# Linear attention and a gated feed-forward layer on one core: the first 900 steps in a new order, and a last store on another queue

## The chip, the cores and the metric

The kernel runs on one core of one Trainium2 chip. The metric is the device time of one execution, in microseconds (us); the profile is of one execution of its own. In the profile PE is TensorE's matrix unit (PEld its weight loads), DVE is VectorE, ACT is ScalarE, POOL is GpSimd and SP is SyncE, which here only issues transfers.

## The reference

Eight heads of linear attention make x, and x goes through a gated feed-forward layer. Cut to what is computed:

```python
# q, k, v: (8 batches, 8 heads, 576 rows, 64)
q_s = softmax(q, over the 64)            # exp(q - max) / (sum + 1e-9)
k_s = softmax(k, over the 576 rows)
kv  = einsum('bhsd,bhse->bhde', k_s, v)
x   = einsum('bhsd,bhde->bhse', q_s, kv) # to (4608 tokens, 512)
xn  = x / sqrt(mean(x * x) + 1e-6) * rms_g
g   = xn @ w_gate                        # (512, 1536)
out = (g * sigmoid(g) * (xn @ w_val)) @ w_out
```

## The kernel before

The 4,608 tokens are nine blocks of 512. The first three (j = 0, 1, 2) go through the layer one after the other, the last six in pairs, by Strassen's products. All products are in float32r: an operand is split into a high and a low part, and three products are added. One program on one core does all of it, and its whole order is written out by hand: `ORDER` is a string of 3,337 steps such as `k_tr.0.2` or `q_sub0.0.3:P`, each a small function with its indices; a letter behind the colon sets the engine (S, A, D, P for SyncE, ScalarE, VectorE, GpSimd). Each engine works through its own instructions in that order, and semaphores hold it where an operand is not ready. Transfers are issued by SP in the same order, a few by ScalarE.

The steps that matter here, with their lines:

- `constants` (435) fills the identity and `mean_w` on GpSimd; `warm` (473) issues TensorE products of `mean_w` that nothing reads. I call them idle products.
- k's softmax needs the maximum over rows. `k_load` (494) loads a pair of heads (b, g); `k_max0` (544, batch 0) or `k_max` (541) take maxima on VectorE; `k_tr` (550, line 554 or 557) turns them on TensorE; `k_top` (560) reduces them on VectorE; `k_rows` (564) turns the result back over all rows; `k_sub` (573) and `k_exp` (577) follow, `k_mm` (588 or 594) multiplies by v with a column of ones, and `k_eps` (612), `k_rec`, `kv_norm0` or `kv_hi` (620) and `kv_lo` divide by the sum. `v_load` (525, 529, 530) loads v, and `kv_zero` (610), `kv_zero0` (606) and `v_ones` (534, 536, 537) fill tiles on GpSimd.
- q's softmax in blocks 0 and 1: `q_load0` (678), `q_max0` (684), `q_sub0` (688), `q_exp` (751), `q_sum0` (693), `q_eps0` (423 or 421), `q_rec0` (700), `q_mul0` (704), `q_t0` (711, four turnings on TensorE), `q_c0`, `q_x0` (724). In block 2 the steps are `q_max` (730), `q_half` (735), `q_max2` (743), `q_sub` (747), `q_sum` (761), `q_half2`, `q_sum2`.
- `n_y0`, `n_y1` (873 to 875, nine small VectorE operations, 128x16 each) and `n_rows` (879) make 1/rms of a block.
- The layer: `load_w` (450), then `conv_mul`, `conv_low`, `conv_shift`, `conv_add` turn weights from float64 words to float32; `w_hi`, `w_lo` (922), `o_hi`, `o_lo` (930) split them; `f1.s.a` (1005) is 12 products into one of two `ps_gv` buffers for chunk s = 12 j + i, with a = 0 for the gate and 1 for the value; `g_mul` (1010) and `h_mul` (1017) read them on VectorE and so free them, `silu` (1014) stands between; `f2` (1042) multiplies by `w_out` into the four `ps_o` banks. `w_keep`, `o_keep`, `s_keep` (990) and `store` (1049) issue transfers out.
- The end: `e_add`, `e_tr`, `e_copy` (409) and `e_put` (1443) bring the last four quarter tiles, 128 KB each, to the output.

The tiles of k have two buffers (`kt`), so a `k_load` waits until the `k_mm` two loads before it has read its tile:

```python
kt = ap.tile([KP, 2, CH, D], F32, name="kt")   # bufs=2
```

Of the kernel before, what the change touches and what calls it, by code (L numbers as in the profile page):

```python
# [27 lines left out]
v_load.0.2 q_eps0.0.1:A q_sub0.0.0:P q_exp.0.0 conv_mul.1.1 q_max0.0.3 k_rows.0.1 k_sub.0.1 q_sum0.0.0 k_exp.0.1
q_exp.0.2 q_eps0.0.0:D k_mm.0.0 k_eps.0.0:D conv_shift.1.1 warm.2.23 q_rec0.0.1 q_mul0.0.1:P conv_low.0.1.1 k_load.1.0
load_w.0.2 warm.2.11 q_rec0.0.0 k_sub.0.3 k_exp.0.3 k_rec.0.0 warm.2.12 q_sum0.0.2 q_eps0.0.2:A k_rows.0.2 k_sub.0.2  # L30
q_load0.1.0 v_ones.0.3 k_mm.0.1 k_eps.0.1:A conv_mul.0.1 warm.2.21 q_sub0.0.3:D load_w.2.1 k_rec.0.1 warm.2.22
q_rec0.0.2 q_exp.0.3 load_w.1.0 warm.2.5 k_mm.0.3 q_mul0.0.0:P q_t0.0.0 conv_mul.0.0 q_load0.1.1 load_w.3.0 load_w.2.0
q_mul0.0.2:P kv_norm0.0.0:D k_exp.0.2 k_eps.0.3:A q_t0.0.1 conv_low.0.0.1 kv_norm0.0.1:D conv_shift.0.1 conv_add.0.1.1
conv_shift.0.0 load_w.4.1 load_w.1.2 q_c0.0.0:A kv_zero0.1 q_sum0.0.3 q_eps0.0.3:D warm.2.13 q_rec0.0.3 q_c0.0.1:A
q_load0.1.2 k_mm.0.2 k_eps.0.2:A conv_mul.0.2 q_x0.0.0 k_max.1.0 conv_add.0.0.1 k_rec.0.3 kv_norm0.0.3:D warm.2.24
load_w.4.0 w_hi.0.0.2:A x_sq.0.0 k_tr.1.0 q_mul0.0.3:D q_t0.0.3 load_w.3.2 q_c0.0.3:A q_x0.0.1 k_rec.0.2 q_max0.1.0
kv_norm0.0.2:D conv_low.0.2.1 conv_shift.0.2 q_t0.0.2 x_hi.0.0:A q_x0.0.3 k_top.1.0 k_rows.1.0 w_lo.0.0:P x_hi.0.1:D
x_lo.0.1 q_c0.0.2:A q_sub0.1.0:P q_exp.1.0 warm.2.25 x_sq.0.3 k_sub.1.0 x_lo.0.0 conv_add.0.2.1 q_max0.1.1 x_sq.0.1
q_x0.0.2 x_sq.0.2 kv_zero.5 q_sum0.1.0 conv_mul.1.0 conv_shift.1.0 w_lo.0.1:P x_hi.0.2:A x_lo.0.2 q_sub0.1.1:P
x_hi.0.3:A n_sum0.0 q_eps0.1.0:A x_lo.0.3 n_sum0.1 kv_zero.1 n_sum0.2 n_sum0.3 warm.2.9 f1.0.0.0.0 f1.0.0.0.1  # L40
v_load.1.0 conv_low.1.0.2 q_rec0.1.0 conv_add.1.0.2 kv_zero.7 f1.0.0.0.2 f1.0.0.0.3 f1.0.0.1.0 k_exp.1.0 q_mul0.1.0:P
conv_mul.2.0 f1.0.1.0.0 f1.0.0.1.1 f1.0.1.0.1 o_hi.0:A conv_low.2.0.2 load_w.3.1 f1.0.0.1.2 o_lo.0:P k_load.1.1
f1.0.1.0.2 w_hi.1.0.2:A w_lo.1.0:P n_t.0 n_y0.0 f1.0.0.1.3 f1.0.0.2.0 f1.0.1.0.3 conv_low.1.2.1 conv_shift.2.0
f1.0.0.2.1 f1.0.0.2.2 f1.0.1.1.0 f1.0.0.2.3 conv_mul.2.1 n_y1.0 n_rows.0 g_mul.0 conv_shift.2.1 f1.0.1.1.1 f1.0.1.1.2
f1.0.1.1.3 conv_mul.1.2 load_w.2.2 conv_shift.1.2 conv_add.1.2.1 f1.0.1.2.0 f1.0.1.2.1 f1.0.1.2.2 k_load.1.2
w_lo.1.1:D kv_zero.0 f1.1.0 q_exp.1.1 conv_mul.4.0 q_sum0.1.1 conv_mul.4.1 conv_shift.4.1 g_mul.1 f1.0.1.2.3 silu.0
k_mm.1.0 conv_shift.4.0 q_eps0.1.1:A k_eps.1.0:D o_hi.1:A conv_mul.3.0 conv_add.2.0.2 load_w.6.0 h_mul.0 q_rec0.1.1
f1.1.1 h_hi.0:A q_t0.1.0 w_hi.2.0.2:A h_lo.0:P load_w.6.1 f2.0 load_w.5.1 k_rec.1.0 kv_norm0.1.0:D conv_mul.3.1 silu.1
q_mul0.1.1:P load_w.4.2 q_c0.1.0:A conv_shift.3.0 conv_low.3.0.2 w_lo.2.1:D q_max0.1.2 conv_shift.3.1 w_lo.2.0:D
f1.2.0 q_load.2.0 conv_mul.2.2 conv_low.4.0.2 conv_add.3.0.2 kv_zero.3 q_sub0.1.2:D exp_table o_lo.1:P conv_mul.6.0  # L50
w_hi.3.0.2:A h_mul.1 w_lo.3.0:P h_hi.1:A h_lo.1:P conv_add.4.0.2 q_exp.1.2 load_w.5.0 conv_shift.2.2 kv_hi.1.0:D
k_max.1.1 w_lo.3.1:P g_mul.2 q_x0.1.0 x_hi.1.0:D q_sum0.1.2 silu.2 x_lo.1.0 q_eps0.1.2:D conv_low.2.2.1 conv_shift.6.0
conv_mul.6.1 conv_shift.6.1 conv_mul.3.2 q_load0.1.3 x_sq.1.0 f1.2.1 h_mul.2 conv_low.4.2.1 conv_mul.5.1
conv_add.2.2.1 conv_shift.3.2 load_w.7.1 f2.1 conv_shift.5.1 q_rec0.1.2 f1.3.1 load_w.7.0 conv_low.3.2.1
conv_add.3.2.1 q_max.2.0 v_load.1.1 conv_mul.4.2 conv_shift.4.2 kv_zero.6 o_hi.2:A o_lo.2:D q_half.2.0 q_mul0.1.2:P
f1.3.0 load_w.5.2 q_max0.1.3 load_w.8.1 h_hi.2:A h_lo.2:D conv_mul.5.0 k_tr.1.1 conv_shift.5.0 g_mul.3 k_top.1.1
w_hi.4.0.2:A w_lo.4.0:D w_lo.4.1:D conv_low.6.0.2 conv_mul.7.0 q_max2.2.0 conv_shift.7.0 conv_low.5.0.2 o_hi.3:A
# [1429 lines left out]
```

## Time and profile before

| | us |
|---|---|
| median of 3 runs (932.59 to 933.10) | 932.92 |
| the profiled execution itself | 932.95 |
| its span, first to last instruction | 930.7 |
| TensorE busy (99% of the span) | 920.5 |
| VectorE busy (78%) | 727.0 |
| GpSimd busy (56%) | 522.4 |
| ScalarE busy (50%) | 461.4 |

2.25 us of the profiled execution lie outside the span. In the profile's 40 slices of 23.3 us TensorE shows 8 in the first and the last and 9 (90% or more) in all the others, and the granted clock is 9 throughout; the chain of work that ended last is TensorE for 95% and VectorE for 3%. A share over the whole says little here: what idle time TensorE has stands in a few places, and the rows of the section below are taken from them.

### The profile page before, as it was taken

Reading aid. Unit: us, or ns where it says so; the run is one execution under the profiler, and the core shown is the slowest. Engines: PE = TensorE matmul, PEld = TensorE weight load, DVE = VectorE, ACT = ScalarE, POOL = GpSimd, SP = SyncE. Lnnn points to the kernel's source line nnn. Section 1 sums busy time; section 2 is a strip of 40 time slices with the busy share of each in tenths; the row PEclk is TensorE's granted clock in tenths of the full one; section 3 lists DMA queues with packets and bytes.
Section 4 is the critical chain, followed back from the end, with each engine's and each line's share of the span. In section 5 each row is a group of like instructions: output and inputs, shape, how many; then the busy total and the mean of one; then the engine's idle time right before and its main releaser. Section 6 shows DMA issues by size and latency. Waiting matters only on the chain.

```text
span 930.7 us, 14213 instructions
## 1 busy us (share of the span) xinstructions
PE 920.5 (99%) x4621; PEld 748.1 (80%) x4621; DVE 727.0 (78%) x1520; ACT 461.4 (50%) x741; POOL 522.4 (56%) x539
## 2 busy tenths in 40 slices
...
GB/s 266 281 268 195 161 90 252 316 275 323 244 221 188 257 246 244 253 255 210 246 211 204 240 274 277 280 304 284 202 184 182 210 195 285 267 185 181 69 158 91
DMA packets 216569, 211.06 MB, mean 227 GB/s; under 512 B 138416, under 2 KB 177840, under 8 KB 211888
## 3 DMA queue, kind: packets, MB, share of 16 engines
...
q14 instruction: 36, 0.29, 0.1%
...
## 4 chain that ended last, share of the span: by engine, by line
PE 95%; DVE 3%; DMA 1%; issue 0%; ACT 0%; POOL 0%; DVEq 0%; ACTq 0%; POOLq 0%
PE ps_gv L1005 20%; PE ps_gv L1154 18%; PE ps_o L1154 12%; PE ps_o L1042 10%; PE ps_a L1154 7%; PE ps_o L1363 6%; PE ps_o L1247 4%; PE ps_a L1363 4%; PE ps_gv L1363 3%; PE ps_a L594 2%; PE ps_a L802 2%; PE ps_a L1247 2%; PE ps_gv L1247 2%; PE ps_o L802 1%; PE ps_gv L476 1%; DMA wd<-w 1%
## 5 line engine op out<-in xcount | busy, mean ns | idle before, releaser
L1005 PE MATMUL ps_gv<-xh,w 128*128 128x512 f32 x576 | 190.6, 397 | 1.3 <-DVE gs L1017 1.3
L1154 PE MATMUL ps_gv<-x,ring 128*128 128x512 f32 x576 | 143.0, 392 | 0.0
L1005 PEld LDWEIGHTS ps_gv<-xh,w 128*128 128x128 f32 x576 | 108.2, 188 | 26.0 <-DVE gs L1017 1.4
L1154 PEld LDWEIGHTS ps_gv<-x,ring 128*128 128x128 f32 x576 | 107.0, 188 | 23.0
L1005 PE MATMUL ps_gv<-xl,w 128*128 128x512 f32 x288 | 112.3, 391 | 0.0
L1175 DVE TENSOR_TENSOR tmp<-tmp,ps_gv 128x512 f32<-128x512 f32 x84 | 57.3, 684 | 49.6 <-PE ps_gv L1154 48.1
L1154 PE MATMUL ps_o<-x,ring 128*128 128x512 f32 x360 | 85.1, 389 | 0.0
L1127 POOL DMA_DIRECT2D ring<-wd x54 | 31.0, 575 | 91.3 <-PE ps_o L1154 34.1
L1154 PEld LDWEIGHTS ps_o<-x,ring 128*128 128x128 f32 x360 | 67.6, 188 | 14.2
L1042 PE MATMUL ps_o<-o,hh 128*128 128x512 f32 x288 | 73.1, 396 | 0.0
L1005 PEld LDWEIGHTS ps_gv<-xl,w 128*128 128x128 f32 x288 | 54.2, 188 | 10.6 <-issue 0.4
L1042 PEld LDWEIGHTS ps_o<-o,hh 128*128 128x128 f32 x288 | 53.0, 188 | 11.3 <-issue 0.4
L1175 DVE TENSOR_TENSOR tmp<-tmp,ps_o 128x512 f32<-128x512 f32 x42 | 28.7, 685 | 29.1 <-PE ps_o L1154 26.0
L409 ACT CAST hh<-gs 128x512 fp32r<-128x512 f32 x48 | 29.6, 616 | 31.7 <-DVE gs L1017 17.4
L1127 POOL DMA_DIRECT2D w<-wd x18 | 10.1, 559 | 58.2 <-PE ps_a L1154 37.9
L922 POOL TENSOR_TENSOR w<-w,w 128x512 fp32r<-128x512 f32 x29 | 39.3, 1363 | 5.1 <-ACT w L409 5.0
L1042 PE MATMUL ps_o<-o,hl 128*128 128x512 f32 x144 | 38.7, 391 | 0.0
L1154 PE MATMUL ps_a<-x,w 128*128 128x512 f32 x144 | 36.9, 392 | 0.0
L541 DVE TENSOR_REDUCE cm<-kt 128x128 f32<-128x640 f32 x28 | 36.7, 1310 | 0.1
L1154 PE MATMUL ps_a<-x,ring 128*128 128x512 f32 x144 | 36.7, 390 | 0.0
L1026 POOL TENSOR_TENSOR hl<-gs,hh 128x512 fp32r<-128x512 f32 x21 | 28.2, 1343 | 14.9 <-ACT hh L409 9.0
L1154 PE MATMUL ps_gv<-x,w 128*128 128x512 f32 x144 | 35.1, 391 | 0.0
...
## 6 DMA issues: line engine op xcount, KB each, us to landing
...
```

The lines of the kernel that those rows point to most:

```text
L409: (e.copy if e is nc.scalar else e.tensor_copy)(dst, src)
L541: nc.vector.tensor_reduce(out=cm, in_=kt_[b, g].rearrange("p h j d -> p h d j"), axis=AX.X, op=ALU.max)
L802: nc.tensor.matmul(px[:, c0:c1], lhsT=wt, rhs=mv[:, c0:c1], start=(i == 0), stop=(i == 2))
L922: on(nc.gpsimd).tensor_tensor(out=w[:, :, 1], in0=halves(CHUNK[s], a, 1)[:, 0], in1=w[:, :, 0].bitcast(F32), op=ALU.subtract)
L1005: nc.tensor.matmul(pd[s], lhsT=w[:, a, c // 2, m, c % 2 * P:c % 2 * P + P], rhs=X[j, c][x], start=(n == 1), stop=(n == 3 * NKT))
L1026: on(nc.gpsimd).tensor_tensor(out=hl, in0=g_[s], in1=h_[s][0].bitcast(F32), op=ALU.subtract)
L1042: nc.tensor.matmul(po[t], lhsT=a[:, t * P:(t + 1) * P], rhs=w, start=(i == 0 and n == 0), stop=(i == NF - 1 and n == len(terms) - 1))
L1127: nc.gpsimd.dma_start(t, src.rearrange("p a b f -> p (a b f)"))
L1154: nc.tensor.matmul(abc[p, i, m, b], lhsT=src[:, h, c * P:(c + 1) * P], rhs=operand(o, c, x), start=first and n == 0, stop=n == 5, skip_gro ...
L1175: nc.vector.tensor_tensor(out=dst, in0=ux[u + (src,)], in1=abc[u + (b,)], op=ALU.add)
L1247: nc.tensor.matmul(pa[p, t, k], lhsT=a[:, k * P:(k + 1) * P], rhs=w, start=(c == 0 and n == 0), stop=(c == NF - 1 and n == 2))
L1363: nc.tensor.matmul(qacc[p, b, x], lhsT=ws[l][x], rhs=h[m], start=first and i == 0 and n == 0, stop=i == NH - 1 and n == 2, skip_group_chec ...
```

## The change

`ORDER` is rewritten up to about step 900 of 3,337 (f1.18.0, near 200 us), and one step at the very end gets another engine. No step is added or left out, and the functions are the same; the string is one line longer, so every line number of the functions is higher by one. Of the table the diff shows the first lines and the last:

```diff
 ORDER = """
-kv_zero.4 k_load.0.0 v_ones.0.0 kv_zero0.0 g_load constants warm.2.2 warm.2.4 warm.2.7 warm.2.6 v_ones.1.1 k_max0.0.0
-warm.2.3 k_load.0.2 k_tr.0.0 k_top.0.0 k_max0.0.2 k_load.0.1 warm.2.8 k_max0.0.1 k_tr.0.2 warm.2.0 k_load.0.3
+q_load0.0.1 constants warm.2.2 warm.2.4 warm.2.6 k_load.0.0 k_load.0.2 warm.2.21 k_max0.0.0 warm.2.0 v_ones.0.0
+warm.2.3 k_max0.0.2 k_tr.0.2 k_top.0.2 k_tr.0.0 k_top.0.0 kv_zero.4 k_load.0.3 warm.2.7 g_load k_load.0.1 k_max0.0.3
...
-e_tr.0.0 e_tr.0.1 e_copy.0.0:A e_add.1.0 e_copy.0.1:A e_tr.1.0 e_put.0.0:S e_add.1.1 e_tr.1.1 e_put.0.1:S e_copy.1.0:D
+e_tr.0.0 e_tr.0.1 e_copy.0.0:A e_add.1.0 e_copy.0.1:A e_tr.1.0 e_put.0.0:S e_add.1.1 e_tr.1.1 e_put.0.1:A e_copy.1.0:D
 e_copy.1.1:A e_put.1.0:S e_put.1.1:S
```

These steps stand on another engine than before: q_sub0.0.3 and q_sub0.1.2 on GpSimd in place of VectorE; q_eps0.0.0, q_eps0.1.2, k_eps.1.1, k_eps.1.2, h_hi.7, h_hi.9 and x_hi.1.3 on ScalarE in place of VectorE; q_eps0.0.1, k_eps.0.1, q_eps0.1.1, h_hi.11, q_hi.2.0, kv_hi.2.0 and kv_hi.2.2 on VectorE in place of ScalarE; h_lo.10 on VectorE in place of GpSimd; e_put.0.1 on ScalarE's queue in place of SP's.

**TensorE, from its first instruction to the first product with v.** L476 are the idle products, L554 a k_tr (three turnings), L567 a k_rows, L588 a k_mm; `w_92` holds k's maxima. Before:

```order
L476 MATMUL ps_gv<-mean_w 128x512 x10
L554 MATMUL ps_o<-ident,w_92 128x96 x3
L476 MATMUL ps_gv<-mean_w 128x512 x2
L554 MATMUL ps_o<-ident,w_92 128x96 x3
L476 MATMUL ps_gv<-mean_w 128x512 x4
L567 MATMUL ps_o<-ident,kx 96x128
L554 MATMUL ps_o<-ident,w_92 128x96 x3
L476 MATMUL ps_gv<-mean_w 128x512 x2
L554 MATMUL ps_o<-ident,w_92 128x96 x3
L476 MATMUL ps_gv<-mean_w 128x512 x11
L567 MATMUL ps_o<-ident,kx 96x128 x2
L588 MATMUL ps_o<-w_93,w_94 64x128 x12
```

And with the change:

```order
L477 MATMUL ps_gv<-mean_w 128x512 x12
L555 MATMUL ps_o<-ident,w_92 128x96 x6
L477 MATMUL ps_gv<-mean_w 128x512 x4
L568 MATMUL ps_o<-ident,kx 96x128
L477 MATMUL ps_gv<-mean_w 128x512 x2
L555 MATMUL ps_o<-ident,w_92 128x96 x3
L477 MATMUL ps_gv<-mean_w 128x512 x13
L555 MATMUL ps_o<-ident,w_92 128x96 x3
L477 MATMUL ps_gv<-mean_w 128x512 x4
L568 MATMUL ps_o<-ident,kx 96x128
L477 MATMUL ps_gv<-mean_w 128x512 x2
L589 MATMUL ps_o<-w_93,w_94 64x128 x12
```

Twelve idle products stand ahead of the first turning in place of ten, two k_tr follow each other, and the last k_tr and the k_rows behind it have moved behind more of the idle products.

**VectorE, from block 1's 1/rms to k's second subtraction of batch 2.** L573 is a k_sub (`kt_1276` is head pair 2.0, `kt_1558` is 2.1), L873 to L875 are one of n_y1's three rounds (the other two are left out), L743 is q_max2.2.2, L879 n_rows.1, L562 k_top.2.1, L1010 g_mul.12. Before:

```order
L867 TENSOR_SCALAR y_1741<-ps_a_1680 128x16
L573 TENSOR_TENSOR kt_1276<-kt_1276,ps_a_1686 128x640
L873 SCALAR_TENSOR_TENSOR ps_a_1680<-y_1741,ps_a_1680 128x16
L874 TENSOR_TENSOR ps_a_1680<-ps_a_1680,y_1741 128x16
L875 SCALAR_TENSOR_TENSOR y_1741<-ps_a_1680,y_1741 128x16
L743 TENSOR_REDUCE sw_1774<-st_1571 128x16
L879 STREAM_TRANSPOSE r_1776<-y_1741 128x512
L562 TENSOR_REDUCE kx_1782<-ps_a_1769 128x1
L1010 TENSOR_TENSOR gs_1784<-ps_gv_1688,r_1776 128x512
L573 TENSOR_TENSOR kt_1558<-kt_1558,ps_a_1769 128x640
```

And with the change (`kt_1272` is 2.0, `kt_1595` is 2.1):

```order
L868 TENSOR_SCALAR y_1738<-ps_a_1674 128x16
L874 SCALAR_TENSOR_TENSOR ps_a_1674<-y_1738,ps_a_1674 128x16
L875 TENSOR_TENSOR ps_a_1674<-ps_a_1674,y_1738 128x16
L876 SCALAR_TENSOR_TENSOR y_1738<-ps_a_1674,y_1738 128x16
L574 TENSOR_TENSOR kt_1272<-kt_1272,ps_a_1683 128x640
L880 STREAM_TRANSPOSE r_1775<-y_1738 128x512
L1011 TENSOR_TENSOR gs_1777<-ps_gv_1690,r_1775 128x512
L762 TENSOR_REDUCE sum_1_1780<-qt_1306 128x16
L563 TENSOR_REDUCE kx_1785<-ps_a_1783 128x1
L574 TENSOR_TENSOR kt_1595<-kt_1595,ps_a_1783 128x640
```

n_y1 has moved ahead of k_sub.2.0, g_mul.12 ahead of k_top.2.1, and q_sum.2.1 has come in between.

**SP's queue, at the loads of k and v for batch 2.** L501 and L503 are a k_load (`kt_1825` is 2.2, `kt_1908` is 2.3), L529 and L530 a v_load, L990 a store of parts, L948 a w_keep, L952 an o_keep, L1049 a store of the output. Before:

```order
L501 DMA kt_1825<-in_k_dram 128x2x256
L503 DMA kt_1825<-in_k_dram 128x2x64
L990 DMA wd1_105<-parts_1723 128x2x512
L529 DMA vt_1845<-in_v_dram 128x4x64 x2
L530 DMA vt_1845<-in_v_dram 64x2x64
L1049 DMA out_0_dram<-ot_1860 128x512
L501 DMA kt_1908<-in_k_dram 128x2x256
L503 DMA kt_1908<-in_k_dram 128x2x64
```

And with the change (`kt_1827` is 2.2, `kt_1831` is 2.3):

```order
L502 DMA kt_1827<-in_k_dram 128x2x256
L504 DMA kt_1827<-in_k_dram 128x2x64
L949 DMA wd5_109<-w_1600 128x2x1024
L502 DMA kt_1831<-in_k_dram 128x2x256
L504 DMA kt_1831<-in_k_dram 128x2x64
L991 DMA wd1_105<-parts_1725 128x2x512
L1050 DMA out_0_dram<-ot_1868 128x512
L1050 DMA out_0_dram<-ot_1875 128x512
L953 DMA od11_121<-o_1679 128x1024
L530 DMA vt_1835<-in_v_dram 128x4x64 x2
L531 DMA vt_1835<-in_v_dram 64x2x64
```

k_load.2.3 now stands ahead of v_load.2.2, and so do two stores of the output and an o_keep.

## Rows read from the trace of the kernel before

**Rows 1.** Stretch, length; busy us of PE, PEld, DVE, ACT, POOL; clock, DMA, GB/s.
```profile
10.00:20.00 10.00, 10.00 (x84) 7.74 (x84) 9.69 (x20) 6.33 (x12) 5.88 (x8) 1.00 1.10 292
20.00:30.00 10.00, 8.83 (x77) 5.99 (x77) 9.55 (x24) 7.99 (x16) 7.54 (x7) 1.00 1.07 316
...
36.00:140.00 104.00, 104.00 (x530) 83.62 (x529) 90.37 (x176) 81.50 (x121) 86.06 (x74) 1.00 0.62 184
140.00:160.00 20.00, 17.96 (x113) 14.19 (x112) 16.97 (x47) 14.24 (x22) 13.26 (x17) 1.00 0.71 251
```

**Rows 2.** Timeline of POOL's first us: start, us, what, [idle before, releaser].
```profile
0.73 0.34 POOL L610 MEMSET kv<- 128x128 f32 x2 [0.29 <-POOLq L1472]
...
1.56 0.20 POOL masks.py:197 MEMSET ident<- 128x128 f32 x1
```

**Rows 3.** Timeline of PE: the first idle products.
```profile
2.33 4.64 PE L476 MATMUL ps_gv<-mean_w 128*128 128x512 f32 x10 [2.33 <-POOL vt L536]
```

**Rows 4.** Timeline of DVE, 3 to 27 us: k's maxima, q_sub0.0.3, a kv_norm0, q_mul0.0.3.
```profile
3.85 0.55 DVE L547 TENSOR_TENSOR w<-w 96x384 f32<-96x384 f32 x1 [3.85 <-DMA w<-in_k_dram]
7.49 0.46 DVE L562 TENSOR_REDUCE kx<-ps_o 128x1 f32<-128x288 f32 x1 [3.08 <-PE ps_o L554]
...
19.45 0.86 DVE L688 TENSOR_TENSOR r<-r,st 128x512 f32<-128x512 f32 x1
...
25.73 0.58 DVE L416 TENSOR_SCALAR ot<-ps_o,rs 64x64 f32<-64x64 f32 x2
26.32 0.69 DVE L704 TENSOR_TENSOR xl<-r,sm 128x512 f32<-128x512 f32 x1
```

**Rows 5.** Timeline of SP's issues: six of q's loads.
```profile
3.21 2.83 SPq L678 DMA_DIRECT2D qt<-in_q_dram  x6
```

**Rows 6.** Timeline of PE: q_t0.0.3, and the first real products.
```profile
27.16 0.63 PE L711 MATMUL ps_o<-ident,xl 128*128 128x128 f32 x4 [1.17 <-DVE rs L618]
...
35.56 1.07 PE L1005 MATMUL ps_gv<-xh,w 128*128 128x512 f32 x4
```

**Rows 7.** Timeline of PE, 150 to 158 us: k_tr.2.1, k_rows.2.1, k_mm.2.1, f1.13.1.
```profile
150.59 0.27 PE L557 MATMUL ps_a<-ident,cm 128*128 128x128 f32 x1
151.60 0.32 PE L567 MATMUL ps_a<-ident,kx 128*128 128x128 f32 x1 [0.74 <-DVE kx L562]
...
155.54 0.80 PE L594 MATMUL ps_a<-vt,kt 128*64 128x65 f32 x20
157.63 0.50 PE L1005 MATMUL ps_gv<-xh,w 128*128 128x512 f32 x1 [1.29 <-DVE gs L1017]
```

**Rows 8.** Timeline of DVE, 144 to 156; last, L922's min/median/max in ns, 36 to 160.
```profile
144.55 0.66 DVE L761 TENSOR_REDUCE sum<-qt 128x16 f32<-128x512 f32 x1
...
148.01 0.82 DVE L573 TENSOR_TENSOR kt<-kt,ps_a 128x640 f32<-128x640 f32 x1 [2.28 <-PE ps_a L567]
148.75 0.17 DVE L873 SCALAR_TENSOR_TENSOR ps_a<-y,ps_a 128x16 f32<-128x16 f32 x1
...
150.66 0.71 DVE L879 STREAM_TRANSPOSE r<-y 128x512 f32<-128x512 f32 x1
...
154.38 1.76 DVE L922 TENSOR_TENSOR w<-w,w 128x512 fp32r<-128x512 f32 x1
...
L922 DVE TENSOR_TENSOR w<-w,w x13: 677/693/1756, 41.7 to 154.4; 128x512 fp32r<-128x512 f32 x13
```

**Rows 9.** v_load.2.2's first issues, landing of v's six (156 to 170), k_mm.2.2.
```profile
156.77 1.97 SPq L529 DMA_DIRECT2D vt<-in_v_dram  x2
...
DMA to landing us min/median/max: 4.0/5.6/6.2
...
169.88 0.80 PE L594 MATMUL ps_a<-vt,kt 128*64 128x65 f32 x20
```

**Rows 10.** The last four issues on SP; ScalarE's own issues before, ns.
```profile
926.34 1.99 SPq L1443 DMA_DIRECT2D out_dram<-res  x4
...
L1409 ACTq DMA_DIRECT2D out_dram<-res x8: 322/430/672, 914.3 to 921.6; - x8
```

More of the change, by code (lines that the diff above doesn't have):

```diff
@@ L28 @@
[L28 to L57, printed above, removed]
@@ L83 @@
-silu.11 v_ones.2.0 v_load.2.0 q_load.2.3 o_hi.11:D n_sum.1 h_mul.11 o_lo.11:D kv_lo.1.2:P k_tr.2.0 f1.12.0 q_hi.2.0:A
-q_sub.2.1:P w_keep.12:S r_keep.5 kv_lo.1.3:P q_exp.2.1 f1.12.1 r_keep.2 s_add.1.1:D r_keep.0 n_t.1 s_add.1.2:P
-h_hi.11:A k_top.2.0 s_hi.1.1:A q_sum.2.1 h_lo.11:P k_rows.2.0 s_hi.1.2:A n_y0.1 f2.11 k_sub.2.0 n_y1.1 k_exp.2.0
-o_keep.12:S k_tr.2.1 store.0.0:A q_max2.2.2 n_rows.1 q_sub.2.2:P store.0.2:A k_top.2.1 g_mul.12 k_rows.2.1 s_lo.1.1:P
-k_mm.2.0 q_exp.2.2 k_sub.2.1 w_keep.13:S w_hi.14.0.2:A r_keep.1 f1.13.0 k_eps.2.0 q_half2.2.1 s_add.1.4:P k_load.2.2
```

184 lines of the change are left out of this document (110 added, 74 removed).

## The prediction, before the change was run

> **What bounds the kernel now.** I read the time by stretch first, then the early stretch engine by engine, then the one late stretch in which TensorE is idle, and last the end. By stretch [rows 1], TensorE is not idle at all from 10 to 20 us, for 1.17 between 20 and 30, not at all from 36 to 140 (104.00 of 104.00), and for 2.04 between 140 and 160. The reader should see that what the change reorders ends near 200 us, that TensorE's work is the same in both kernels, and that the time can therefore only move by TensorE's idle time in three places: before its first product (2.33 [rows 3]), before q's last turnings of the first block, and in 140 to 160. The granted clock is 1.00 in all these stretches; still the first ten products take 4.64 us [rows 3].
>
> At the start TensorE waits until 2.33 for POOL, which fills `kv`, a stripe of ones and `ot` (from 0.73) before it starts on the identity at 1.56 [rows 2, 3]. VectorE then sits idle for 3.08 us until k's first maxima are turned at 7.49 [rows 4]: its first maximum was done at 4.40, but the turning stood behind the ten idle products. From there to 27 us VectorE is the bound: 9.69 and 9.55 of 10 us busy [rows 1]. The 1.17 us that TensorE waits until 27.16 end with VectorE's chain, in which q_mul0.0.3 (26.32) is the last large piece [rows 4, 6]. From 27.16 to the first real product at 35.56 [rows 6] TensorE is almost without idle time, so that start moves with 27.16.
>
> **The change, part by part.** It leaves every step in, puts about the first 900 of 3,337 in a new order, and gives 18 another engine, one of them a store.
>
> *Start, POOL and TensorE.* The constants now come first on POOL: 1.56 less 0.73, 0.83 us earlier [rows 2], so the first idle product starts at about 1.50 in place of 2.33. But twelve idle products now stand ahead of the first turning, not ten: at 0.46 us each (4.64 by ten [rows 3]) that gives back 0.93, so TensorE comes to it at 7.0, as before. And two of q's loads are now issued ahead of k's on SP: at 0.47 each (2.83 for six [rows 5]) they put k's first landing from 3.85 to 4.8 or later [rows 4], and the first turning now needs the second k load, which lands after that. Gain here: nothing. VectorE does two k maxima ahead of its first reduction, not one, and is ahead by that one, 0.55 [rows 4]. I let it be lost again: thirteen idle products now stand ahead of k_tr.0.1, where two did since the turning before, and VectorE's k_eps.0.0 now waits for k_mm.0.0, which comes behind another six.
>
> *Start, VectorE.* Up to q_mul0.0.3 VectorE loses q_sub0.0.3 (0.86 [rows 4], to POOL) and gains k_eps.0.1 (some 0.15, as small as its other steps on one column); q_eps0.0.0 and q_eps0.0.1 swap engines and cancel. That is 0.71 us less in a chain that is full, so q_mul0.0.3 ends 0.7 earlier and TensorE's wait of 1.17 shrinks to about 0.5. POOL takes the subtraction where it is idle; its cover is gone if q_mul0's steps on POOL come later by it, at most the 0.86 itself. Bounds of the whole start: 0 if the idle products eat it, 2.0 (0.83 + 1.17) if TensorE's earlier start and the whole wait come through. I take **0.6**, near VectorE's 0.71, since its chain is what ends last there.
>
> *36 to 140.* No idle time before; the moved steps (q_sub0.1.2 to POOL, h_hi.7 and h_hi.9 to ScalarE, eps steps) cost nothing as long as TensorE's operands stay ahead of it. Where one doesn't, the price is a wait like those in the late stretch, 0.7 to 1.3 [rows 7]. I count 0 and let the range hold one half of such a wait.
>
> *140 to 160.* Before, VectorE stands idle for 2.28 us until k_rows.2.0 lets k_sub.2.0 run at 148.01, and only then does n_y1's nine small operations and one more (148.75 to 150.66); k_top.2.1 and g_mul.12 stand behind them [rows 8]. TensorE waits 0.74 for k_top.2.1, and 1.29 for h_mul.12, until 157.63 [rows 7]. Now the ten run inside the idle 2.28. k_top.2.1 can run as soon as k_tr.2.1 has (150.59 + 0.27), so the 0.74 falls to about 0.3. But f1.13.1 waits for h_mul.12, and from 148.01 to its release is 9.62 us: less 1.91 for the ten, plus q_sum.2.1 (0.66), plus kv_hi.2.0 as a pair on VectorE (0.58, as the pair in [rows 4]), plus q_max2.2.3 (some 0.17), plus about 0.6 of idle time for the trip k_tr, k_top, k_rows that was covered: 9.7. So h_mul.12 gains nothing by count, and the second wait grows by what the first loses. The other bound is w_lo.14.1: it took 1.76 where this operation's median on VectorE is 0.69 [rows 8]; if it runs undisturbed, h_mul.12 comes 1.07 earlier. I take **0.35**, nearer to the count.
>
> The row shows one subtraction of VectorE stretched by 1.07 us. The Trainium skill, SBUF — State Buffer, section "Who interferes with whom", says that a VectorE instruction with two SBUF inputs and a POOL instruction that reads SBUF take turns at a shared port. By that rule the stretch stays as long as POOL adds or subtracts at that time, which the new order still has it do, and this stage's gain would be 0.
>
> *The end.* e_put.0.1 goes to ScalarE's queue. The four last stores take 1.99 us of issuing on SP [rows 10]; with three there the last could be issued up to 0.5 earlier, but ScalarE must issue its store first (0.32 to 0.67 for its other stores [rows 10]) and only then makes the copy that the last store needs. I take **0.1**, bounds -0.2 and 0.5. The Trainium skill, DMA: Bandwidth & Descriptors, section "Issuing engines are not separate DMA queues", says that such a move saves issuing time only, as the transfers share the same engines; by that the end of the transfers would stay where the bytes put it, and the gain would be near 0.
>
> **Sum.** 0.6 + 0.35 + 0.1 = 1.05 us off the profiled execution's own 932.95, which lies 0.03 above the median of the three runs: **931.9 us**, 0.11% less. A measurement of this kernel tells about 0.2% from no change, 1.87 us: below 931.05 is faster, above 934.8 slower.
>
> **The rivals.**
>
> *Faster: TensorE alone is the bound of the start.* It starts 0.83 earlier and the whole wait of 1.17 goes, less some 0.5 for k's later landing: 1.5. w_lo.14.1 runs undisturbed: 1.0 in the late stretch. With the end 2.65: 930.3. For it: the idle products may hide waits that no row shows; against it: VectorE's 9.7 of 10 us.
>
> *No gain: it does not do what it says.* The order shows twelve idle products ahead of the first turning, and sixteen ahead of k_rows.0.0, as many as before; k lands later. Then 27.16 stays, the late stretch gives 0.1 and the end 0.1: 932.7.
>
> *Slower: SP's queue stands behind k_load.2.3.* It now comes ahead of a store of parts, two stores of the output, o_keep.13 and v_load.2.2, and its buffer is free only when k_mm.2.1 is done (155.54 + 0.80 [rows 7]). Before, v_load.2.2 was issued from 156.77 [rows 9]. The queue would go on at 156.4 with two k issues, the parts and three stores; at 0.5 to 1.0 an issue (0.99 for v's first two [rows 9]) v's three issues lie between 159.4 and 165.4, and the last lands 4.0 to 6.2 later [rows 9]: 163.4 to 171.6. k_mm.2.2 needs it at 169.88 [rows 9], 1 us sooner if the gains above come. It decides once v lands after that; at 171.6 TensorE stands 2.7 us, and if none of the gains come the time is 935.6, with them 934.6. I price it at 935.0. For it: issues are slow there; against it: the middle of the bounds, 167.5, is still in time.
>
> **How the numbers follow.** Forecast 0.48 (its own spread 931.0 to 932.8); faster rival 0.25; no gain 0.17; slower rival 0.10. Faster by over 0.2%: the faster rival and a little of the forecast's lower end, 0.27; slower: most of the slower rival, 0.09; same 0.64. The range leaves out the slower rival and the part of the faster one that lies below its price: 930.1 to 933.3.
>
> **What would show it.** Right: a first product near 1.5; a wait before q_t0.0.3 of about 0.5 and the first real product near 35.0; no idle time from there to 140; in the late stretch a wait of 0.3 before k_rows.2.1 and of 1.3 or more before f1.13.1. Wrong: a first real product before 34.3, or still at 35.5; a wait of TensorE in 36 to 140; a wait of k_mm.2.2 with v's load as its releaser; a w_lo.14.1 of 0.7.

## The result, and the profile after

The changed kernel takes **938.67 us** (median of six runs, 938.18 to 942.10) beside 933.01 for the kernel before in the same runs: a ratio of 1.0063, interval 1.0046 to 1.0080, so slower by 0.6%. The forecast was 931.9 in a range of 930.1 to 933.3. The profiled execution took 938.85 with a span of 936.7, so 6.0 us more span than before. In the later runs the executions of one kernel scatter by up to some 12 us on one chip, so below each ratio comes with its interval, and what an edit does is read from where TensorE's products start in the traces.

The page of the changed kernel, its busy times:

```profile
PE 923.0 (99%) x4621; PEld 748.3 (80%) x4621; DVE 732.6 (78%) x1521; ACT 460.8 (49%) x739; POOL 520.6 (56%) x540
```

The two later stretches of [rows 1], one more behind them, and three short ones (length; busy us of PE, PEld, DVE, ACT, POOL; granted clock, DMA, GB/s):

```profile
36.00:140.00 104.00, 102.92 (x518) 81.15 (x518) 91.77 (x171) 82.82 (x124) 81.21 (x68) 1.00 0.64 190
140.00:160.00 20.00, 18.54 (x116) 14.64 (x114) 17.11 (x39) 10.93 (x15) 15.47 (x22) 1.00 0.57 187
160.00:180.00 20.00, 17.80 (x92) 14.66 (x93) 17.34 (x47) 13.20 (x21) 11.51 (x11) 0.91 0.89 291
...
158.70:162.10 3.40, 0.23 (x8) 0.09 (x4) 3.26 (x8) 0.15 (x1) 2.90 (x4) 1.00 1.05 390
162.10:165.80 3.70, 3.60 (x9) 2.88 (x10) 3.53 (x15) 2.37 (x5) 1.54 (x3) 0.54 0.88 313
165.80:170.00 4.20, 4.20 (x20) 3.48 (x19) 2.75 (x5) 3.95 (x6) 3.46 (x3) 1.00 0.75 210
```

36 to 140 now holds 1.08 us in which TensorE is idle, where it held none. And there is something new: a stretch in which TensorE's clock is granted at about half, 0.54 from 162.1 to 165.8, right behind 3.3 us in which it did nothing.

Timeline of PE (start us, us, what, [idle before, releaser]); the lines that answer to [rows 3, 6, 7] and the two in between where it now waits:

```profile
1.50 4.74 PE L477 MATMUL ps_gv<-mean_w 128*128 128x512 f32 x12 [1.50 <-POOL mean_w L438]
7.20 0.71 PE L555 MATMUL ps_o<-ident,w 96*128 96x96 f32 x6 [0.95 <-DVE w L548]
...
27.41 0.63 PE L712 MATMUL ps_o<-ident,xl 128*128 128x128 f32 x4 [1.16 <-DVE xl L705]
...
69.22 0.32 PE L568 MATMUL ps_a<-ident,kx 128*128 128x128 f32 x1 [0.19 <-DVE kx L563]
...
115.32 1.19 PE L1043 MATMUL ps_o<-o,hl 128*128 128x512 f32 x4 [0.50 <-DVE hl L1027]
...
154.19 0.32 PE L568 MATMUL ps_a<-ident,kx 128*128 128x128 f32 x1 [0.39 <-DVE kx L563]
...
162.19 0.79 PE L1006 MATMUL ps_gv<-xh,w 128*128 128x512 f32 x1 [3.27 <-DVE gs L1018]
162.78 0.63 PE L1006 MATMUL ps_gv<-xl,w 128*128 128x512 f32 x1
163.21 0.63 PE L1006 MATMUL ps_gv<-xh,w 128*128 128x512 f32 x1
```

The last two lines start 0.43 apart. The same products before start 0.23 apart:

```profile
157.97 0.39 PE L1005 MATMUL ps_gv<-xl,w 128*128 128x512 f32 x1
158.20 0.40 PE L1005 MATMUL ps_gv<-xh,w 128*128 128x512 f32 x1
```

DVE and POOL in the trace of the changed kernel:

```profile
5.33 0.55 DVE L548 TENSOR_TENSOR w<-w 96x384 f32<-96x384 f32 x1 [5.33 <-DMA w<-in_k_dram]
6.59 0.55 DVE L548 TENSOR_TENSOR w<-w 96x384 f32<-96x384 f32 x1 [0.71 <-DMA w<-in_k_dram]
...
26.57 0.69 DVE L705 TENSOR_TENSOR xl<-r,sm 128x512 f32<-128x512 f32 x1
...
109.75 2.91 DVE L923 TENSOR_TENSOR w<-w,w 128x512 fp32r<-128x512 f32 x1 [1.19 <-ACT w L410]
...
114.58 0.68 DVE L1027 TENSOR_TENSOR hl<-gs,hh 128x512 fp32r<-128x512 f32 x1
...
157.76 2.72 DVE L923 TENSOR_TENSOR w<-w,w 128x512 fp32r<-128x512 f32 x1
160.51 0.69 DVE L736 TENSOR_REDUCE st<-st 32x16 f32<-32x16 f32 x4
161.23 0.19 DVE L744 TENSOR_REDUCE sw<-st 128x16 f32<-128x32 f32 x1
161.45 0.69 DVE L1018 TENSOR_TENSOR gs<-ps_gv,gs 128x512 f32<-128x512 f32 x1
```

```profile
109.57 1.29 POOL L931 TENSOR_TENSOR o<-w,o 128x512 fp32r<-128x512 f32 x1
110.82 1.29 POOL L923 TENSOR_TENSOR w<-w,w 128x512 fp32r<-128x512 f32 x1
...
157.43 2.50 POOL L979 TENSOR_TENSOR sums<-w 128x512 f32<-128x512 f32 x2
...
159.94 1.66 POOL L979 TENSOR_TENSOR sums<-w 128x512 f32<-128x512 f32 x1
```

w_lo.14.1 (157.76) takes 2.72 where it took 1.76 in [rows 8], and ends at 160.48, 0.55 behind the second of two POOL additions in a row (157.43 + 2.50 = 159.93). h_mul.12 (161.45) stands behind it, and f1.13.1 waits for h_mul.12. The same happened to w_lo.9.1 at 109.75: 2.91, over two POOL operations in a row, to 112.66, 0.55 behind their end at 112.11. h_lo.7 (114.58) stands behind that one and is what f2.7 waits for at 115.32. Before, w_lo.9.1 took 0.82:

```profile
107.15 0.82 DVE L922 TENSOR_TENSOR w<-w,w 128x512 fp32r<-128x512 f32 x1 [1.28 <-ACT w L409]
```

I call this a hold: a VectorE operation with two inputs in SBUF stands until an operation of POOL is done. It is not new with the change. Each of the two kernels has some 305 such operations of 128x512, with a median of 0.68 us; 40 of them take over 0.9 before, and 41 with the change. Of the 288 operations of this size with an input in PSUM, the buffers that TensorE writes, none takes over 0.70.

Where the 6.0 us come from, by the start of the same product in both traces (worked out from the two timelines of PE):

```
product                        before    after    later by    new here
f1, at 45 us                    44.63    44.98     +0.35       +0.35   start
f1, at 63 us                    63.05    63.42     +0.38       +0.03
f1, at 78 us                    78.05    79.63     +1.58       +1.20   waits between 65 and 73
f2.6's low pass, second        104.61   106.66     +2.06       +0.48   waits at 92 and 106, not taken apart
f2.7's low pass, second        112.77   115.65     +2.88       +0.82   behind w_lo.9.1
k_rows.2.1                     151.60   154.19     +2.59       -0.29   n_y1 in VectorE's idle time
f1.13.1's first                157.63   162.19     +4.56       +1.97   behind w_lo.14.1
f1.13.1's ninth                159.58   165.72     +6.14       +1.58   the clock
end of the span               930.7    936.7       +6.0        -0.1    the last stores
```

By starts a short wait comes to more than the idle time shown: a product is drawn 0.39 long while the next starts 0.23 behind it, which hides some 0.16 of a wait, and the first product behind a wait has the next one 0.33 behind it. So the 0.50 at 115.32 is a loss of 0.77, and the 1.08 us idle from 36 to 140 go with one of 2.5.

### The profile page after: what moved, and what is told of

Its sections match the earlier page's. It is cut to its first block, busy times and chain, and to the rows that moved or that the text cites. A ratio compares the mean times of both kernels' runs of the same rounds, so it can differ in the third digit from the quotient of the medians.

```text
span 936.7 us, 14203 instructions
## 1 busy us (share of the span) xinstructions
PE 923.0 (99%) x4621; PEld 748.3 (80%) x4621; DVE 732.6 (78%) x1521; ACT 460.8 (49%) x739; POOL 520.6 (56%) x540
## 4 chain that ended last, share of the span: by engine, by line
PE 86%; DVE 3%; ACT 1%; issue 1%; ACTq 0%; DVEq 0%
PE ps_gv L1155 18%; PE ps_gv L1006 16%; PE ps_o L1155 12%; PE ps_o L1043 8%; PE ps_a L1155 7%; PE ps_o L1364 6%; PE ps_o L1248 4%; PE ps_a L1364 4%; PE ps_gv L1364 3%; PE ps_a L595 2%; PE ps_a L803 2%; PE ps_a L1248 2%; PE ps_gv L1248 2%; DVE w L923 1%; PE ps_o L803 1%
## 5 line engine op out<-in xcount | busy, mean ns | idle before, releaser
L777 POOL TENSOR_TENSOR qt<-qt,sm 128x512 f32<-128x512 f32 x25 | 27.1, 1086 | 14.3 <-DVE sm L774 11.5
```

The source lines that it names most:

```text
L777: on(nc.vector).tensor_tensor(out=qt_[j, g], in0=qt_[j, g], in1=sm_[j, g].unsqueeze(2).broadcast_to([P, M, 32]), op=ALU.mult)
```

## The experiments

Every kernel here differs in the table of steps alone, and does every step once; a splice takes one kernel's steps up to a point and the rest in the other's order. Each is compared with the kernel before on its own chip, and profiled.

### Which part loses: start, middle, late

```diff
 e1_start:  steps ahead of f1.0.0.0.0 as changed, the rest as before
 e5_mid:    as before; from f1.0.0.0.0 to f1.11.0 as changed; then as before
 e2_late:   as before up to f1.11.0, then as changed (store e_put.0.1 on SP)
 e14_36_60: as before; from f1.0.0.0.0 to f1.3.0 as changed; then as before
```

> The changed order up to the first product of f1 (chunk 0), the order of before from there on; ScalarE's store at the end not taken over. Theory (the loss is made behind the start, above all between 150 and 165 us): the start alone gives what the two traces show there, first product 0.83 earlier but xl's last piece 0.25 later and f1 0.4 later, so 933.4, and no wait of TensorE over 0.1 between 36 and 140. Rival (a late start pushes every later step of VectorE, and the waits between 65 and 79 and at 114 follow from it): those waits appear here too, 1.5 to 2.5 us in all, 934.9 to 935.9. My forecast of the record: 0.6 less, 932.4.

Measured: ratio 0.9978 (0.9957 to 0.9999), lowest run 932.31 beside 932.33. No wait of TensorE between 36 and 140 as the theory said, and products there start 0.31 earlier than before, not 0.35 later. So a shift of 0.3 at the start is within what one execution differs from the next: the last large piece of VectorE's chain, q_mul0.0.3, starts between 25.47 and 26.32 in six traces that have the start of before (mean 25.93) and between 25.60 and 27.34 in twelve that have the changed one (mean 26.28). The ratio lies just under 1, but the lowest runs are the same, and q_mul0.0.3 comes 0.35 later on average, not 0.7 earlier: a gain of the start is not shown.

> The order of before up to the first product of f1, the changed order from there up to f1 of chunk 11, and the order of before again from there; no store on ScalarE. Theory (36 to 140 loses by its own order, whatever start it has): the waits of the changed kernel between 65 and 73 and at 114 appear here, 1.7 to 2.2 us by the shift of TensorE's products between 60 and 120, and the time is 1.7 to 2.2 above before. Rival (they come from the changed start): under 0.5, as before.

Measured: ratio 1.0022 (0.9995 to 1.0049), lowest 933.78 beside 932.80; in the trace the same products start 0.01 earlier at 45 us and 2.42 later at 115:

```profile
68.79 0.32 PE L568 MATMUL ps_a<-ident,kx 128*128 128x128 f32 x1 [0.20 <-DVE kx L563]
114.85 1.20 PE L1043 MATMUL ps_o<-o,hl 128*128 128x512 f32 x4 [0.49 <-DVE hl L1027]
```

Both waits are there with the start of before. The middle loses by its own order, 2.4 us. Behind it 1.0 comes back at f1.13.1, whose wait falls to 0.2, since h_mul.12 in its old place is then in time, and 1.2 is lost again between 361 and 366, in steps that stand as before; what makes that is open. The span is 933.4, 2.7 above before.

> The order of before up to f1 of chunk 11, the changed order from there on, without the store on ScalarE. Theory (VectorE's subtraction w_lo.14.1 is held by POOL's additions and h_mul.12 comes behind it; TensorE's wait then costs it its clock): the wait before f1.13.1 is 2.5 to 3.5 with the granted clock under 0.95 in 160 to 180, and the time 935.5 to 937. Rival (the wait is long only because the changed order arrives there late from 36 to 140): the wait stays within 0.5 of the 1.29 of before, the clock at 1.00, 932.5 to 933.5.

Measured: ratio 1.0035 (1.0012 to 1.0058), lowest 935.16 beside 932.33. The trace, PE and DVE:

```profile
150.38 0.32 PE L568 MATMUL ps_a<-ident,kx 128*128 128x128 f32 x1 [0.39 <-DVE kx L563]
158.39 0.50 PE L1006 MATMUL ps_gv<-xh,w 128*128 128x512 f32 x1 [3.27 <-DVE gs L1018]
```

```profile
153.95 2.72 DVE L923 TENSOR_TENSOR w<-w,w 128x512 fp32r<-128x512 f32 x1
```

The hold, the wait (3.27) and then the low clock (0.59 from 158.3 to 162.3) are the same behind a middle that is the old one: the late part makes them itself. By products it gains 0.35 at k_rows.2.1 and loses 1.97 and 1.60 behind it, 3.2 net; the profiled 935.16 is that less 0.87 by which this execution came earlier out of its first 9 us: its idle products go from 0.43 to 0.23 apart at 5.5 us, while in the trace of before, in the same order, they start 0.43 apart up to the first turning at 6.77.

> The order of before up to the first product of f1, the changed order from there to f1 of chunk 3 (about 36 to 60 us), the order of before again from there. Theory (what TensorE waits for between 65 and 73 is made in 36 to 60): TensorE's waits there are 0.8 to 1.2 in all, as in the changed kernel, and none at 114. Rival (it is made by the order from 60 on): under 0.4.

Measured: ratio 1.0011 (0.9992 to 1.0029). Products start 0.23 earlier at 44 us and 1.20 later at 69:

```profile
65.94 1.89 PE L1042 MATMUL ps_o<-o,hh 128*128 128x512 f32 x7 [0.33 <-DVE o L930]
67.98 1.19 PE L1042 MATMUL ps_o<-o,hl 128*128 128x512 f32 x4 [0.15 <-DVE hl L1026]
69.38 0.32 PE L567 MATMUL ps_a<-ident,kx 128*128 128x128 f32 x1 [0.20 <-DVE kx L562]
```

The waits between 65 and 73 are made by the changed order from 36 to 60 us, and come out 10 us behind it. There is no wait at 114.

### The hold at 157.76, and the clock

```diff
 e4_pool, POOL's part of the order:
-v_ones.2.2 s_add.2.1:P ... s_add.0.1:P ... s_add.0.3:P kv_lo.2.0 h_lo.12:P
+v_ones.2.2 ... kv_lo.2.0 h_lo.12:P s_add.2.1:P s_add.0.1:P s_add.0.3:P
```

> The changed kernel with three additions of POOL (s_add.2.1, s_add.0.1, s_add.0.3) put behind h_lo.12 on POOL; VectorE's order is untouched. Theory (a VectorE subtraction with two SBUF inputs stands still while POOL adds): w_lo.14.1 takes 0.7 in place of 2.72, h_mul.12 comes 2.0 earlier, TensorE's wait before f1.13.1 is 1.0 to 1.5, the clock stays at 1.00, and the time is 938.7 - 2.0 - 1.6 = 935.1 (934.6 to 935.6). Rival (w_lo.14.1 is slow by itself, by its operands): it stays over 1.7 and the time within 0.7 of 938.7.

Measured: ratio 1.0030 (1.0007 to 1.0053). The trace of DVE, and of PE:

```profile
157.47 0.69 DVE L923 TENSOR_TENSOR w<-w,w 128x512 fp32r<-128x512 f32 x1
159.13 0.69 DVE L1018 TENSOR_TENSOR gs<-ps_gv,gs 128x512 f32<-128x512 f32 x1
```

```profile
159.88 0.50 PE L1006 MATMUL ps_gv<-xh,w 128*128 128x512 f32 x1 [1.24 <-DVE gs L1018]
169.00 0.30 PE L558 MATMUL ps_a<-ident,cm 128*128 128x128 f32 x1 [0.65 <-DVE cm L542]
```

Nothing of VectorE's order was touched, and the same subtraction takes 0.69: it was POOL that held it. The wait is 1.24 and the clock 1.00 from 160 to 180, and TensorE is 3.9 us earlier at 166 than in the changed kernel (0.3 of it from the start). But 2.1 of it is given back by 183: k_max.2.2 (0.65) and a kv step (0.32) of VectorE, which is now busy for 19.54 of the 20 us from 160 to 180, are waited for next. Part of that busy time is the hold again. The three additions now run beside s_lo.1.2 and s_lo.1.4, which stand ahead of k_max.2.2 and took 0.68 and 0.63 in the changed kernel:

```profile
163.57 1.78 DVE L988 TENSOR_TENSOR parts<-sums,parts 128x512 fp32r<-128x512 f32 x1
...
165.44 1.62 DVE L988 TENSOR_TENSOR parts<-sums,parts 128x512 fp32r<-128x512 f32 x1
```

The profiled time is 937.08, 1.8 below the changed kernel, not 3.6.

```diff
 e3_hmul:
-q_half2.2.1 w_lo.14.1:D q_half.2.3 q_max2.2.3 h_mul.12
+q_half2.2.1 h_mul.12 w_lo.14.1:D q_half.2.3 q_max2.2.3
```

> The changed kernel with h_mul.12 ahead of w_lo.14.1 on VectorE, nothing else moved. Theory: h_mul.12 starts when silu.12 is done, 158.3 in place of 161.45, TensorE's wait before f1.13.1 falls from 3.27 to 0.3 to 0.8, the granted clock stays at 1.00 in 160 to 180, and the time falls by the wait's 2.5 to 3.0 and the clock's 1.6: 934.0 to 934.7. Rival (the clock falls there for another reason than this wait): the wait falls but the clock stays under 0.95, 935.8 to 936.4. Rival (VectorE is late there whatever stands first): the next product waits instead, 938 or more.

Measured: ratio 1.0055 (1.0030 to 1.0079), profiled 937.11.

```profile
159.06 0.50 PE L1006 MATMUL ps_gv<-xh,w 128*128 128x512 f32 x1 [0.20 <-DVE gs L1018]
169.69 0.30 PE L558 MATMUL ps_a<-ident,cm 128*128 128x128 f32 x1 [2.16 <-DVE cm L542]
```

f1.13.1's wait is gone, and the clock stays at 1.00, as the theory said. The wait is then found at k_tr.2.2, 2.16 us, on k_max.2.2. The subtraction behind h_mul.12 takes 1.51 there, but right ahead of k_max.2.2 VectorE is idle, since q_sum.2.3 waits for ScalarE's q_exp.2.3:

```profile
167.68 0.69 DVE L762 TENSOR_REDUCE sum<-qt 128x16 f32<-128x512 f32 x1 [1.45 <-ACT qt L752]
```

The second rival is right that the next product waits. The profiled time falls by 1.7, which is neither the theory's 4 nor the rival's 938 or more, and by its ratio this kernel is not told apart from the changed one.

Three kernels in which TensorE idles by 2.2 us at most there (these two and e10_both, below) keep the clock. In all eight with 3.26 to 3.28 (the changed one, and seven that leave this place as it is) it falls to about half behind the wait. How long it stays there differs. In the changed kernel it is 0.91 on average from 160 to 180, in e7_hlo10 0.83. By products that is 1.6 us there and 2.7 here, for the same wait: five of the eight lose 1.6, and e7_hlo10, e15_qeps and e16_shift 2.7 to 2.8.

```diff
 e12_hold, the kernel before:
-k_mm.2.1 v_ones.2.2 w_lo.14.1:D kv_hi.2.0:A q_half.2.3 s_add.2.1:P
+k_mm.2.1 s_add.2.1:P v_ones.2.2 w_lo.14.1:D kv_hi.2.0:A q_half.2.3
```

> The kernel of before with one step moved on POOL: s_add.2.1 ahead of v_ones.2.2, so that POOL's next addition follows w_lo.14.0 at once. Theory (VectorE's w_lo.14.1 runs only once POOL's run of two-input operations has a gap): it takes 3.0 in place of 1.76, ends 0.55 after POOL's second operation, h_mul.12 comes 1.2 later, TensorE's wait before f1.13.1 is 2.5 in place of 1.29, the time 1.2 above before, and more if the clock falls. Rival (VectorE takes its turn as soon as POOL's first operation ends): 1.76 stays, POOL's s_add.2.1 is stretched by 0.4 instead, the time within 0.3 of before.

Measured: ratio 0.9987 (0.9955 to 1.0019). DVE, then POOL:

```profile
153.79 1.74 DVE L922 TENSOR_TENSOR w<-w,w 128x512 fp32r<-128x512 f32 x1
```

```profile
153.70 1.29 POOL L922 TENSOR_TENSOR w<-w,w 128x512 fp32r<-128x512 f32 x1
154.94 1.72 POOL L978 TENSOR_TENSOR sums<-w 128x512 f32<-128x512 f32 x1
```

The theory's form was too simple, and the rival is right: VectorE took its turn as the first POOL operation ended, and the second was stretched from 1.29 to 1.72. That a second operation follows at once is not enough for a second hold. What decides who gets the turn stays open.

### The middle: which moved steps

```diff
 e9_wlo9:  -w_lo.9.1:D      +w_lo.9.1:P
 e10_both: e4_pool and e9_wlo9 together
 e7_hlo10: -h_lo.10:D       +h_lo.10:P
```

> The changed kernel with w_lo.9.1 on POOL in place of VectorE, where it took 2.91 us at 109.75 (0.68 is what this operation takes undisturbed). Theory (held behind two operations of POOL, it made h_lo.7 late): VectorE comes to h_lo.7 1.0 to 2.0 earlier, the 0.50 wait before f2.7's low pass goes, TensorE is 0.6 to 0.9 earlier at 120 us; since h_mul.12's time is set by VectorE's own list, the wait before f1.13.1 grows by about as much, and the whole time is within 0.6 of the changed kernel. Rival (h_lo.7 is late for silu or the low words on ScalarE): the wait stays.

Measured: ratio 1.0036 (1.0008 to 1.0064). The wait at 115 is gone; against the changed kernel TensorE is 1.05 earlier at 108 us by that execution's start, and 1.82 at 115, so w_lo.9.1 was worth **0.77**. What the theory said of the end is wrong: the next wait, before f1.13.1, is 3.27 as before the edit, so the gain is kept. VectorE's list there waits for TensorE itself (k_top.2.1 for k_tr.2.1, k_sub.2.1 for k_rows.2.1) and moves with it.

> The changed kernel with both holds taken away: w_lo.9.1 on POOL, and s_add.2.1, s_add.0.1, s_add.0.3 behind h_lo.12 on POOL. Theory: no operation of VectorE over 1.8 us at 105 to 115 and 155 to 162, the clock at 1.00 throughout, and a profiled time 1.8 (the second alone gave that) to 2.6 below the changed kernel's, 936.2 to 937.0; the rest to before is the 1.1 of TensorE's waits between 65 and 73 and what VectorE's list still costs at 150 to 185. Rival (the two losses are one and the same): as with the second alone, 937.0 to 937.3.

Measured: ratio 1.0014 (0.9987 to 1.0041), profiled 937.65. Neither hold is there and the clock is 1.00, but TensorE waits 0.90 at 115 all the same, because ScalarE stood for the third weights of a chunk:

```profile
112.93 0.66 ACT L458 ACTIVATE raw<-raw 128x512 int32<-128x512 uint32 x1 [1.85 <-DMA raw<-in_moe_w_out_dram]
```

That load lands at 112.91 in this execution, 110.00 in e9's, 111.06 in the changed kernel's and 107.80 before; its issue on SP is at 102.05 before and 105.43 changed. So the changed order also spends the margin of this load, and whether that costs differs from one execution to the next. The time is above what the theory and its rival gave, and the sum of the two edits was not shown.

> The changed kernel with h_lo.10 back on POOL, as in before. Theory: the wait of 0.50 before the low pass of f2 at 114 goes with what follows it, TensorE is 0.5 to 0.8 earlier at 130 us. Rival (POOL is later than VectorE there): the wait grows to over 0.7.

Measured: ratio 1.0070 (1.0042 to 1.0098); the wait at 115 is there as before. I had named the wrong step: what waits there is h_lo.7, behind w_lo.9.1.

```diff
 e13_qsub:  -q_sub0.1.2:P    +q_sub0.1.2:D
 e6_whi:    -w_hi.4.0.2:A kv_zero.6 ... h_hi.2:A h_lo.2:D
            +kv_zero.6 ... h_hi.2:A h_lo.2:D w_hi.4.0.2:A
 e15_qeps:  -q_eps0.1.1:D    +q_eps0.1.1:A
 e16_shift: -conv_mul.3.0 conv_add.2.0.2 ... q_rec0.1.1 conv_shift.3.0
            +conv_mul.3.0 conv_shift.3.0 conv_add.2.0.2 ... q_rec0.1.1
```

> The changed kernel with q_sub0.1.2 back on VectorE, as in before. Theory (on POOL its 1.04 us at 49.75 puts the addition of weights behind it back by 1.06, from 50.06 to 51.12, ScalarE's conversions follow later, and VectorE then stands idle for 2.1 us between 58 and 63 waiting for them): that idle time falls under 1.2, the waits of TensorE between 65 and 73 fall from 1.2 in all to under 0.5, and TensorE is 0.7 to 1.2 earlier at 80 us. Rival (ScalarE is late by its own order, so VectorE gets work without getting time): the waits stay within 0.3 of what they were.

> The changed kernel with w_hi.4 on ScalarE put behind h_hi.2, nothing else moved. Theory: h_hi.2 is done at 65.0 in place of 65.9, so the first product of f2.2 waits no more (0.3), h_lo.2 and k_top.1.1 come earlier on VectorE and the waits behind them (0.4 before k_rows.1.1, 0.35 before f1.4.0) shrink to under half; TensorE is 0.6 to 1.0 earlier at 80 us, and since it is late again at h_mul.12 only by VectorE's own list, part of that may be given back there. Rival (VectorE is late by itself from 63 on): the 0.3 goes and the 0.75 stays.

> The changed kernel with q_eps0.1.1 back on ScalarE, as in before. Theory (its 0.42 us on VectorE at 46.04 puts conv_shift.3.0 back, and ScalarE's next conversion waits for that one's buffer): conv_shift.3.0 is 0.4 earlier, ScalarE's wait of 0.59 at 48.32 shrinks to about 0.2, TensorE's waits between 65 and 73 (1.2 in all) shrink by 0.3 to 0.5. Rival (one such step is absorbed; the order around it makes the delay): they shrink by under 0.15.

> The changed kernel with conv_shift.3.0 on VectorE right behind conv_mul.3.0 in the order, so ahead of the five small steps of block 1's first key and query. Theory (ScalarE's next conversion waits for this step's buffer, and the delay is carried to 65): conv_shift.3.0 starts 1.1 to 1.3 earlier, ScalarE waits for nothing at 48, and TensorE's waits between 65 and 73 shrink by 0.6 or more. Rival (VectorE is full from 39 to 52, so what is put ahead is paid behind): they shrink by under 0.2.

Measured, by where products start against the changed kernel: e13_qsub unchanged between 45 and 115; e6_whi, e15_qeps and e16_shift 0.25, 0.26 and 0.25 earlier at 66, each the one wait at 65.7, and the 0.9 at 69 and 72 unchanged. Their ratios are 1.0063 (1.0043 to 1.0084), 1.0061 (1.0040 to 1.0082), 1.0078 (1.0044 to 1.0113) and 1.0072 (1.0047 to 1.0097), not told apart from the changed kernel's. In e6_whi's trace the 0.25 is lost again by 68, at the low pass behind it; in e15_qeps's and e16_shift's it lasts, and is lost at 166 to a longer low clock. At 115 e6_whi loses 0.41 more, to the late load of weights seen in e10_both. The theories of all four fail: the rivals hold for e13_qsub and e6_whi, and the other two lie between theory and rival. So the step that went from VectorE to POOL costs nothing, as the prediction had it, and no single step of these makes the 0.9. Some of the many that stand in another order between 36 and 60 make it together, and they were not taken apart further.

### A version from the better halves

```diff
 e8_two, the kernel before:
-f2.11 k_sub.2.0 n_y1.1
+f2.11 n_y1.1 k_sub.2.0
-v_ones.2.2 w_lo.14.1:D ... store.0.3:A h_mul.12
+v_ones.2.2 h_mul.12 w_lo.14.1:D ... store.0.3:A
 e11_best: e8_two behind f1.0.0.0.0, the changed start ahead, e_put.0.1:A
```

> The kernel of before with two steps moved on VectorE: n_y1 ahead of k_sub.2.0, h_mul.12 ahead of w_lo.14.1. Theory: n_y1 runs in the 2.28 us in which VectorE stands idle, the wait before k_rows.2.1 falls from 0.74 to 0.3 to 0.4, h_mul.12 starts as silu.12 ends and the wait before f1.13.1 falls from 1.29 to 0.3 to 0.6, if k_max.2.2 and v do not come late for it; the time is 0.9 to 1.4 below before. Rival (VectorE is full up to 170, so what is moved is waited for there): k_tr.2.2 waits by 1 us or more, and the time is within 0.5 of before.

> The changed order up to the first product of f1 and its store on ScalarE, the order of before between, with n_y1 ahead of k_sub.2.0 and h_mul.12 ahead of w_lo.14.1. Theory (the parts add up): 0 to 0.3 at the start, 0.6 in the late stretch, 0.2 at the end: 0.8 to 1.1 below before by the lowest runs, 0.1% and under what medians here can show. Rival (a later stretch gives it back): within 0.3.

Measured: e8_two 0.9996 (0.9970 to 1.0021), lowest 932.04 beside 932.80; e11_best 0.9975 (0.9947 to 1.0003), lowest 931.95 beside 932.13, spans 930.2 and 930.0 beside 930.7. e8_two's PE:

```profile
151.01 0.32 PE L567 MATMUL ps_a<-ident,kx 128*128 128x128 f32 x1 [0.38 <-DVE kx L562]
155.95 0.50 PE L1005 MATMUL ps_gv<-xh,w 128*128 128x512 f32 x1 [0.20 <-DVE gs L1017]
164.68 0.30 PE L557 MATMUL ps_a<-ident,cm 128*128 128x128 f32 x1 [0.23 <-DVE cm L541]
165.17 0.47 PE L802 MATMUL ps_a<-qh,kv 128*128 128x256 f32 x2 [0.19 <-DVE kv L638]
```

Of the 2.04 us of waits in [rows 7] 0.58 are left, but 1.0 of the 1.45 gained by 156 is given back at 165 and 166. What stays is 0.4 by products; no ratio here tells it from nothing. By the lowest runs e8_two lies between its theory and its rival, and e11_best is 0.18 below before, so its rival ("within 0.3") holds: the gains were not shown to add up.

## Why the prediction was wrong

The sum had 1.05 us less, and the span is 6.0 longer. By the table the start loses 0.35 where 0.6 was to be gained, 36 to 140 loses 2.5 where 0 was counted, the late stretch loses 3.3 where 0.35 was to be gained, and the end gains 0.1 to 0.2 where 0.1 was forecast. Two signs that the prediction named for being wrong came: waits of TensorE in 36 to 140, and a first real product no earlier than before, at 36.06.

**36 to 140: "I count 0".** This step failed, by 2.5 us. The working said that moved steps cost nothing as long as TensorE's operands stay ahead, and took the 104.00 of 104.00 in [rows 1] for a margin. It is none: a row of full busy time says that nothing is late, and nothing of how nearly. The half of one wait that the range allowed for is far less than the 1.2 between 65 and 73 and the 0.82 at 115. e5_mid and e14_36_60 show that the order makes them, e9_wlo9 that 0.77 is one VectorE subtraction held over two POOL operations. Which steps between 36 and 60 make the 1.2, and what makes the 0.48 between 78 and 105, stays open.

**"h_mul.12 gains nothing by count."** This step failed too, and with the clock below it is the larger miss, 3.6 us. The count gave 9.7 us from k_sub.2.0's start to f1.13.1; it is 162.19 - 151.01 = 11.18. Of the 1.5 that are missing 0.96 are the hold's growth from 1.76 to 2.72 (e4_pool shows whose it is); the other 0.5 is spread over the small steps ahead of h_mul.12, some 0.1 each. I had bounded the hold on one side alone, by what it would give if it went. The Trainium skill's rule that I cited (SBUF — State Buffer, "Who interferes with whom") agrees with the kind of it, as e4_pool's 0.69 shows. That section says that issue order decides who blocks. The traces differ there: w_lo.9.1 (109.75) stands also through a POOL operation that starts behind it, at 110.82. I cited the rule to say that no gain is to be had, and did not ask what it does when two POOL operations stand in a row.

**The clock was in no term.** A wait was priced at its length. Behind the 3.27 the low clock cost 1.6 more, and 2.7 to 2.8 in three other kernels with the same wait. The Trainium skill, TensorE: Matmul & The Clock Gate, section "Loop structure matters more than you think", has it that TensorE goes cold over long waits between products. The rows at 158.7 and 162.1 agree: 0.54 is about the lower of its two levels (1.2 GHz of 2.4). With it the wait is a loss of 3.6 us over before, not 2.0.

**The start, 0.6.** The first product came at 1.50 and k's first maximum at 5.33 ("4.8 or later"), as forecast. The first turning came at 7.20 ("7.0, as before"), but that is luck: twelve idle products were to take until 7.0, and they were done at 6.24; TensorE then waited 0.95 for k's second maximum. But the "0.71 us less in a chain that is full" did not come through: q_mul0.0.3 starts at 26.57 beside 26.32, and 0.35 later on average over the traces. The chain holds less work, but in it VectorE waits for transfers that come later: 0.71 at 6.59 and 0.31 at 9.30 for loads of k, 0.43 at 11.25 for one of q. From 10 to 20 us it is busy for 9.33 us where it was 9.69 [rows 1]. So the lower bound, 0, was near the case, though it was set for another reason ("if the idle products eat it"), and the sum had taken 0.6.

**What was right.** The wait before k_rows.2.1 fell to 0.39 ("about 0.3"). f1.13.1's was to be 1.3 or more, which says little of 3.27. v_load.2.2 held nothing up, so the slower rival did not occur; it was given 0.10, and what did occur had no chance of its own. The end gained 0.2 where 0.1 was forecast: from the end of the last product to the end of the span it is 3.55 to 3.57 in the eleven traces with a store on ScalarE and 3.77 to 3.78 in the seven without. Three issues on SP take 1.72 where four took 1.99 [rows 10]:

```profile
932.51 1.72 SPq L1444 DMA_DIRECT2D out_dram<-res  x3
932.79 0.40 ACTq L1444 DMA_DIRECT2D out_dram<-res  x1
```

So three of the four terms had the wrong size, by the same habit: what was full, idle or of some length in the rows of before was taken to stay so.
